# Decode attention with a gated MLP: the MLP's weights loaded first, its gate made ahead of the query projection

## The chip, the cores and the metric

The kernel runs on one core of one Trainium2 chip. The metric is the device time of one execution in microseconds (us), as the median of several runs. A core has engines that run side by side, each with its own instruction stream: TensorE (PE in the profile) for matmuls, VectorE (DVE), ScalarE (ACT), GpSimd (POOL) and SyncE (SP), which here does nothing but issue transfers. Transfers from memory are carried by 16 DMA engines.

## The reference

One step of decoding for 8 sequences, in float32: attention over a cache of 4096 keys and values with 32 query heads on 8 key/value heads, and beside it a small MLP whose output, through a silu, multiplies the attention's output.

```python
xn = _layernorm(x)                                  # x: 8 x 1 x 512
# attention: 32 query heads, 8 key/value heads, 128 wide, 4096 positions
q = (xn @ wq) per head
p = softmax(q @ k_cache^T * 128 ** -0.5)
s = (p @ v_cache) over all heads @ wo               # 8 x 1 x 512
# MLP, F = 1792, Fh = 896
z = _gelu(xn @ w_in)                                # tanh form
z1, z2 = z[..., :Fh], _layernorm(z[..., Fh:])
g = w_sp * z2 + b_sp                                # w_sp, b_sp: one number each
y = (z1 * g) @ w_out
return x + s * _silu(y)
```

The caches are 2 x 134 MB, wq and wo 8.4 MB each, the MLP's weights 5.6 MB. Each byte is used once.

## The kernel before, in words

Three slots of 64 KiB in each of the 128 partitions (`slot_a`, `slot_b`, `slot_c`, 8.39 MB each) take all large transfers. For each of the 8 key/value heads h there are four loads that fill a slot: the keys of sequences 0 to 3 (`kT[h, 0]`, into slot a) and of 4 to 7 (`kT[h, 1]`, slot b), then the values in the same two halves (`v[h, 0]` into a, `v[h, 1]` into b). In this text K0 and K1, V0 and V1 are these four of head 0. Slot c holds wq first, and wo at the end. The MLP's weights share slot b with K1: `w_in`, `w_out` and a last block of 128 columns, `side`, of which only two are used (w_sp and b_sp).

`load` (L130) issues a transfer and makes it count up a semaphore as it lands. All large loads stand on SP's queue, written out in the order in which they are to go: wq, the MLP's weights, K0, K1, V0, V1, the same four of every further head, then wo in six pieces and the residual input. A load into a slot that is still read waits on SP for the last reader, and everything behind it waits too. K1 waits for `gate_made`, the last instruction of the MLP, because slot b holds the MLP's weights till then. V0 waits for the step `k0` (the scores of K0 are made), V1 for `k1`; a later head's first half of the keys for `c0`, its second half for `c3`, the steps after which slots a and b have been read.

Ahead of the loop come, in this order on each engine: the layer norm of x and its transposition into `xnT` (L163 to L172); the query projection (L175 to L195), two rounds of 16 matmuls with wq, each followed by a scaling on VectorE into `q_sb`, four transpositions and a copy into `q_all`, and at the end a copy of head 0's queries into `qz`; and the MLP (L198 to L269): a matmul with w_in, a gelu and a layer norm on VectorE with short steps on ScalarE, GpSimd and TensorE, transpositions, a matmul with w_out, a matmul with `pick` that rearranges the result, and the silu, which ends in `gate`. The MLP's intermediates `z`, `u`, `hT`, `y` and `e` are taken by `scratch` from the front of slot c, over wq, which has been read by then. Both parts use the PSUM tiles `t[0]` and `t[1]`.

Matmuls are in float32, and the trace shows each as two passes. VectorE's, ScalarE's and GpSimd's instructions are all recorded on L48, in the helper `op`; all loads on L133.

The loop over heads on TensorE (L311) makes the scores of a half as it lands (`scores`, L290), waits for the softmax on VectorE and ScalarE, transposes the probabilities (L325), and multiplies them with the values of each half (`values`, L300). After the loop come the output projection with wo (L417, L429, L440), the product with the gate and the sum with x.

Of the kernel before, what the change touches and what calls it, by code (L numbers as in the profile page):

```python
# [5 lines left out]
ALU = mybir.AluOpType  # L6
AX = mybir.AxisListType

P = 128
B, D = 8, 512  # L10
HKV, REP, S, DH = 8, 4, 4096, 128
NK = D // P
G = 4
J = S // (G * P)
R = 32
# [11 lines left out]
WO_PIECES = [(0, 18 * D), (18 * D, 26 * D), (26 * D, 28 * D), (28 * D, 30 * D), (30 * D, LAST), (LAST, NWO * D)]  # L27
FOLDED = NWO - REP
N_IN, N_OUT = NK * 2 * FH, NB * D
N_MLP = N_IN + N_OUT + P  # L30


# [26 lines left out]
def build(nc, x, kT, v, wq, wo, w_mlp, x_res, out):  # L59
    def sb(name, shape, align=32):  # L60
        return nc.alloc_sbuf_tensor(name, shape, F32, align_bytes=align).ap()

    slots = [sb(f"slot{i}", [P, SLOT], 512) for i in range(3)]
    slot_a, slot_b, slot_c = slots
    ident = sb("ident", [P, P])
    x_sb = sb("x_sb", [B, D])
    xn = sb("xn", [B, D])
    xnT = sb("xnT", [P, NK, R])
# [5 lines left out]
    q_sb = sb("q_sb", [P, REP * DH])  # L74
    q_all = sb("q_all", [P, HKV, B, REP])
    qz = sb("qz", [P, B * (R + REP)])
    p = sb("p", [P, J, P])
# [12 lines left out]
    def ps(name, shape):  # L90
        return nc.alloc_psum_tensor(name, shape, F32).ap()
# [4 lines left out]
    t = [ps(f"t{i}", [P, 512]) for i in range(2)]  # L96
# [6 lines left out]
    V = Lane(nc, nc.vector, "v_done")  # L103
# [3 lines left out]
    te = nc.tensor  # L107

    class Marks:
        sem = pe_sem  # L110
        n = 0
    PE = Marks()

    def mark(ins):
        ins.then_inc(pe_sem, 1)
        PE.n += 1
        return PE, PE.n

    def pe_wait(*after):
        for lane, n in after:  # L120
            te.wait_ge(lane.sem, n)
# [5 lines left out]
    def landed(key):  # L127
        return Dma(key), 16

    def load(engine, dst, src, key, *after):  # L130
        for lane, n in after:
            engine.wait_ge(lane.sem, n)
        engine.dma_start(dst, src).then_inc(loaded[key], 16)  # L133


    load(nc.scalar, x_sb, x, "x")
    load(nc.sync, slot_c, wq, "wq")
    load(nc.sync, slot_b[:, :N_MLP], w_mlp, "mlp")
    load(nc.sync, slot_a, kT[0, 0], "a")


# [5 lines left out]
    qz_zero = L.op("memset", qz, 0.0, alone=True)  # L147
# [5 lines left out]
         after=[made])  # L153
# [11 lines left out]
    d = V.op("tensor_scalar", rstd[:, 0:1], mv[:, 1:2], EPS, None, op0=ALU.add)  # L165
    d = L.op("tensor_tensor", rstd[:, 1:2], rstd[:, 0:1], neg_half[:B, 0:1], op=ALU.pow, after=[d])
    d = V.op("tensor_scalar", xn, x_sb, mv[:, 0:1], rstd[:, 1:2], op0=ALU.subtract, op1=ALU.mult, after=[d])
    pe_wait(made, d)
    for k in range(NK):
        i = te.transpose(misc[:, k * B:(k + 1) * B], xn[:, k * P:(k + 1) * P], ident[:B, :B])  # L170
    d = V.op("tensor_copy", xnT[:, :, :B], misc[:, :NK * B].rearrange("p (k b) -> p k b", k=NK),
             after=[mark(i), xnT_zero])  # L172


    wq_v = slot_c.rearrange("p (k n) -> p k n", k=NK)  # L175
    pe_wait(landed("wq"), d)
    for quad in range(2):
        for k in range(NK):
            for g in range(G):
                lo = (quad * G + g) * REP * DH  # L180
                i = te.matmul(t[0][R * g:R * (g + 1), :], xnT[:, k, :], wq_v[:, k, lo:lo + REP * DH],  # L181
                              start=(k == 0), stop=(k == NK - 1))
        d = V.op("tensor_scalar", q_sb, t[0], float(DH) ** -0.5, None, op0=ALU.mult, after=[mark(i)])
        pe_wait(d)
        for r in range(REP):
            i = te.transpose(t[1][:, r * P:(r + 1) * P], q_sb[:, r * DH:(r + 1) * DH], ident)
        tv = t[1].rearrange("p (r g c) -> p g c r", r=REP, g=G)
        V.op("tensor_copy", q_all[:, quad * G:(quad + 1) * G], tv[:, :, :B], after=[mark(i)])
    wq_read = PE, PE.n
    qz_v = qz.rearrange("p (b s) -> p b s", s=R + REP)[:, :, :REP]  # L190

    def next_q(h):
        return V.op("tensor_copy", qz_v, q_all[:, h], after=[qz_zero] if h == 0 else [])

    q_ready = next_q(0)  # L195


    spare = [0]  # L198

    def scratch(n):  # L200
        lo = spare[0]
        spare[0] = lo + n
        return slot_c[:, lo:lo + n]

    w_in = slot_b[:, :N_IN].rearrange("p (k a f) -> p k a f", k=NK, a=2)
    w_out = slot_b[:, N_IN:N_IN + N_OUT].rearrange("p (j d) -> p j d", j=NB)
    side = slot_b[:, N_IN + N_OUT:N_MLP]
    z = scratch(2 * FQ).rearrange("p (a f) -> p a f", a=2)
    u = scratch(2 * FQ).rearrange("p (a f) -> p a f", a=2)
    pz = t[0].rearrange("p (a f) -> p a f", a=2)  # L210
    d = V.op("memset", t[0], 0.0)
    pe_wait(landed("mlp"), d)
    for k in range(NK):
        for g in range(G):
            lo = g * FQ
            n = min(FQ, FH - lo)
            i = te.matmul(pz[R * g:R * (g + 1), :, :n], xnT[:, k, :], w_in[:, k, :, lo:lo + n],
                          start=(k == 0), stop=(k == NK - 1))
# [4 lines left out]
    d = V.op("tensor_mul", uf, uf, zf)  # L223
    d = A.op("activation", uf, uf, AF.Tanh, scale=GELU_C, after=[d])
# [15 lines left out]
    d = V.op("tensor_scalar", one["var"], one["var"], EPS, None, op0=ALU.add)  # L240
    d = L.op("tensor_tensor", one["rs"], one["var"], neg_half, op=ALU.pow, after=[d])
    V.op("tensor_scalar", z2, z2, one["rs"], None, op0=ALU.mult, after=[d])
    V.op("tensor_scalar", z2, z2, side[:, 0:1], side[:, 1:2], op0=ALU.mult, op1=ALU.add, after=[landed("mlp")])
    d = V.op("tensor_mul", u[:, 1, :], z2, z1)
    hT = scratch(2 * P).rearrange("p (a s) -> p a s", a=2)
    pe_wait(d)
    for a in range(2):
        i = te.transpose(t[1][:, a * P:(a + 1) * P], u[:, 1, a * P:(a + 1) * P], ident)
    d = V.op("tensor_copy", hT, t[1][:, :2 * P].rearrange("p (a s) -> p a s", a=2), after=[mark(i)])
    pe_wait(d)  # L250
    for j in range(NB):
        g, a = divmod(j, 2)
        i = te.matmul(t[0][R * g:R * (g + 1), :], hT[:, a, R * g:R * (g + 1)], w_out[:, j, :],
                      start=(a == 0), stop=(a == 1 or j == NB - 1))
    mlp_read = mark(i)
    y = scratch(D)
    d = V.op("tensor_copy", y, t[0], after=[mlp_read])
    pe_wait(d)
    py = misc[:, 128:128 + W]
    for g in range(G):  # L260
        for a in range(2):
            i = te.matmul(py[R * g:R * (g + 1), :], pick[:, a, :],
                          y[:, (2 * g + a) * W:(2 * g + a + 1) * W], start=(a == 0), stop=(a == 1))
    e = scratch(W)
    d = V.op("tensor_scalar", e, py, -1.0, 87.0, op0=ALU.mult, op1=ALU.min, after=[mark(i)])
    d = A.op("activation", e, e, AF.Exp, after=[d])
    V.op("tensor_scalar", e, e, 1.0, None, op0=ALU.add, after=[d])
    V.op("reciprocal", e, e)
    gate_made = V.op("tensor_mul", gate, py, e)  # L269


    STEPS = ["k0", "k1", "a", "mm", "tot", "t0", "t1", "v0", "v1", "c0", "v2", "v3", "c3"]
# [2 lines left out]
    def step(h, name):  # L275
        return PE, base + h * len(STEPS) + STEPS.index(name) + 1
# [34 lines left out]
    with te.Fori(0, HKV):  # L311
# [11 lines left out]
        for c in range(2):  # L323
            for j in range(4):
                i = te.transpose(t[c][:, j * P:(j + 1) * P], p[:, 4 * c + j, :], ident)  # L325
# [21 lines left out]
    def softmax(h):  # L347
        nm, l, w, wl = (one[n] for n in ("nm", "l", "w", "wl"))
        V.op("tensor_reduce", nm, sc, op=ALU.max, axis=AX.XY, negate=True, after=[step(h, "k1")])
        give()  # L350
        A.op("activation", p.rearrange("p j s -> p (j s)"), sc.rearrange("p c s -> p (c s)"), AF.Exp,
             bias=nm, accum_out=l, after=[step(h, "a")])
        V.op("tensor_reduce", nmin, misc[:1, :P].rearrange("b (g r) -> b r g", g=G), op=ALU.min, axis=AX.X,
             after=[step(h, "a")])
        V.op("tensor_copy", row, nmin[:, None, :].to_broadcast([1, G, R]))
        give()
        d = V.op("tensor_sub", w, misc[:, 256:257], nm, after=[step(h, "mm")])
        d = A.op("activation", w, w, AF.Exp, after=[d])
        V.op("tensor_mul", wl, w, l, after=[d])
        give()  # L360
        V.op("reciprocal", wl, misc[:, 320:321], after=[step(h, "tot")])
        V.op("tensor_mul", w, w, wl)
        V.op("tensor_scalar", p, p, w, None, op0=ALU.mult)
        give()
        for c in range(2):
            tv = t[c].rearrange("p (j g i e r) -> p e j i g r", j=4, g=G, i=B // 2, e=2)
            for e in range(2):
                V.op("tensor_copy", pT_v[:, 4 * c:4 * c + 4, :, e, e].rearrange("p j i (g r) -> p j i g r", g=G),
                     tv[:, e], after=[step(h, f"t{c}")] if e == 0 else [], alone=(e == 1))
        if h + 1 < HKV:  # L370
            next_q(h + 1)
        give()
# [7 lines left out]
    for h in range(HKV):  # L380
# [13 lines left out]
        else:  # L394
            for a in range(2):
                o_made = V.op("tensor_copy", oT_last[:, :, a, a * B:(a + 1) * B], po_t,
                              after=[step(h, "c3"), oT_zero] if a == 0 else [], alone=(a == 1))


    for i, (lo, hi) in enumerate(WO_PIECES):  # L400
        load(nc.sync, slot_c[:, lo:hi], wo[:, lo:hi], f"wo{i}", *([gate_made] if i == 0 else []))
    load(nc.sync, x_out, x_res, "res")
    wo_v = slot_c.rearrange("p (m d) -> p m d", d=D)
    part, acc = [sc[:, 0, :D // 2], t[0][:, :D // 2]], sc[:, 1, :W]
# [8 lines left out]
    for m in range(FOLDED):  # L413
        h, r = divmod(m, REP)
        need((m + 1) * D)
        for s in range(2):
            i = te.matmul(part[s][R * r:R * r + B, :], oT[:, h, r, :], wo_v[:, m, s * D // 2:(s + 1) * D // 2],  # L417
                          start=(m < REP), stop=(m >= FOLDED - REP))
# [18 lines left out]
    for g in range(G):  # L437
        for a in range(2):
            c = (2 * g + a) * W
            te.matmul(acc[R * g:R * g + OUT_ROWS, :], pick[:, a, :OUT_ROWS], part_f[:, c:c + W],  # L440
                      start=False, stop=False)
# [8 lines left out]
    d = V.op("tensor_add", gate, gate, x_out, after=[landed("res")])  # L450
# [3 lines left out]
    lo, hi = min(s.num for s in used), max(s.num for s in used)  # L454
# [39 lines left out]
```

## Time and profile before

| | |
|---|---|
| median of 3 runs | 688.91 us (688.72 to 689.17) |
| the profiled execution | 687.01 us, its span from the first to the last instruction 685.7 us |
| moved | 290.97 MB, 424 GB/s on average over the span |
| busy share of the span | TensorE 53%, VectorE 17%, ScalarE 2%, GpSimd 1% |
| mean granted TensorE clock | 0.741 of full speed |

A profile here is one execution recorded by the hardware. Its page gives the busy time of each engine, the span cut into 40 slices (17.14 us each) with the busy share in tenths, what the DMA engines moved in each, the chain of work that ended last, and groups of equal instructions. In rows of instructions the first number is the start in us from the span's start, the second the time to the end of the group, then engine, line, operation, the tiles written and read, the count, and in brackets how long the engine had been idle before it and what ended that. Rows of transfers give the median time from issue to landing.

### The profile page before, as it was taken

How to read it: one execution, taken by the hardware profiler on the slowest of the kernel's cores; microseconds unless marked ns; L12 is line 12 of the kernel's file. 1: busy time of each engine (PE TensorE's matmuls, PEld its weight loads, DVE VectorE, ACT ScalarE, POOL GpSimd, SP SyncE). 2: the span in 40 equal slices, each digit the busy share in tenths (PEclk: the TensorE clock that was granted, in tenths of full speed). 3: DMA queues.
4: the chain of work that ended last, by engine and by line, in shares of the span. 5: the costliest groups of instructions: out<-in, count | busy, mean ns of one | idle time of the engine just before them, and what ended most of it. 6: DMA issues, size and time to landing. Idle time of an engine off the chain costs nothing. (4 is left out here: it accounts for less than half of the span.)

```text
span 685.7 us, 5749 instructions
## 1 busy us (share of the span) xinstructions
PE 361.2 (53%) x2544; PEld 124.2 (18%) x2544; DVE 113.7 (17%) x222; ACT 13.8 (2%) x28; POOL 4.2 (1%) x13
## 2 busy tenths in 40 slices
PE   0637255655644465655645365555644455655637
PEld 0112021211311121211211121211211121211313
DVE  3051022200311022200302022200202022200302
ACT  0000000000000000000000000000000000000000
POOL 2000000000000000000000000000000000000000
PEclk9987666677677667767767767767777676677779
DMA  9996999999999999999999999999999999999997
GB/s 418 398 433 264 460 432 425 428 428 432 428 432 428 428 428 459 443 432 428 432 432 428 432 428 428 451 447 436 428 432 429 428 432 432 428 440 459 436 397 293
DMA packets 6072, 290.97 MB, mean 424 GB/s; under 512 B 936, under 2 KB 1064, under 8 KB 1456
## 3 DMA queue, kind: packets, MB, share of 16 engines
q1 hardware_dynamic: 6048, 290.85, 98.2%
q8 instruction: 5, 0.08, 0.0%
q14 instruction: 3, 0.02, 0.0%
q10 hardware_dynamic: 16, 0.02, 0.0%
HBM read 290.83 MB, written 0.03 MB: 424 GB/s over the span
## 5 line engine op out<-in xcount | busy, mean ns | idle before, releaser
L290 PE MATMUL sc<-slot,qz 128*32 128x512 f32 x1024 | 147.9, 742 | 133.1 <-PEq L282 133.1
L300 PE MATMUL o_ps<-slot,pT 128*32 128x512 f32 x1024 | 151.1, 747 | 98.4 <-PEq L282 98.4
L290 PEld LDWEIGHTS sc<-slot,qz 128*32 128x32 f32 x1024 | 40.5, 133 | 234.0 <-issue 234.0
L300 PEld LDWEIGHTS o_ps<-slot,pT 128*32 128x32 f32 x1024 | 44.3, 130 | 186.5 <-issue 186.4
L48 DVE TENSOR_TENSOR o_all<-o_ps,diag 128x512 f32<-128x512 f32 x32 | 22.1, 692 | 203.9 <-PE o_ps L300 203.9
L48 DVE TENSOR_REDUCE nm<-sc 128x1 f32<-128x1024 f32 x8 | 9.8, 1225 | 278.1 <-PE sc L290 278.1
L48 DVE TENSOR_REDUCE o_sb<-o_all 128x128 f32<-128x512 f32 x32 | 33.6, 1051 | 1.1
L325 PE MATMUL t<-ident,p 128*128 128x128 f32 x64 | 15.5, 424 | 11.7 <-PEq L279 11.7
L48 ACT ACTIVATE p<-sc,nm 128x1024 f32<-128x1024 f32 x8 | 8.9, 1113 | 566.8 <-PE misc L317 566.8
L306 PE MATMUL po<-fold,o_sb 128*128 128x8 f32 x64 | 12.4, 266 | 14.2 <-PEq L279 14.2
L181 PE MATMUL t<-slot,xnT 128*32 128x512 f32 x64 | 10.2, 792 | 14.4 <-DMA slot<-in_wq 14.4
L306 PEld LDWEIGHTS po<-fold,o_sb 128*128 128x128 f32 x64 | 9.7, 190 | 35.8 <-issue 35.8
L325 PEld LDWEIGHTS t<-ident,p 128*128 128x128 f32 x64 | 12.6, 224 | 12.1 <-issue 12.1
L48 DVE COPY pT<-t 128x256 f32<-128x256 f32 x32 | 12.1, 419 | 12.0 <-PE t L325 11.2
L317 PE MATMUL misc<-ident,nm 128*1 128x128 f32 x8 | 2.2, 269 | 12.5 <-PEq L279 12.5
L321 PE MATMUL misc<-wl,same 128*128 128x1 f32 x16 | 3.8, 310 | 8.2 <-PEq L279 8.2
L48 DVE TENSOR_SCALAR p<-p,w 128x1024 f32<-128x1024 f32 x8 | 6.0, 753 | 0.3
L181 PEld LDWEIGHTS t<-slot,xnT 128*32 128x32 f32 x64 | 2.3, 137 | 20.4 <-DMA slot<-in_wq 14.5
L48 DVE TENSOR_SCALAR q_sb<-t 128x512 f32<-128x512 f32 x2 | 1.4, 692 | 24.1 <-PE t L181 24.1
L319 PE MATMUL misc<-ident,row 1*128 1x1 f32 x8 | 1.7, 211 | 6.7 <-PEq L279 6.7
L321 PEld LDWEIGHTS misc<-wl,same 128*128 128x128 f32 x16 | 3.4, 265 | 8.7 <-issue 8.7
L231 PE MATMUL misc<-s,same 128*128 128x1 f32 x4 | 1.2, 362 | 7.0 <-DVE s L48 7.0
(79 smaller groups left out, 71.2 us busy)
## 6 DMA issues: line engine op xcount, KB each, us to landing
slot<-in_w_mlp SPq DMA_DIRECT2D x1, 5440.0 KB, 34.1
slot<-in_wo SPq DMA_DIRECT2D x1, 4608.0 KB, 39.4
slot<-in_wo SPq DMA_DIRECT2D x1, 2048.0 KB, 43.8
slot<-in_wo SPq DMA_DIRECT2D x2, 512.0 KB, 45.0
slot<-in_wo SPq DMA_DIRECT2D x1, 384.0 KB, 45.8
slot<-in_kT SPq DMA_DIRECT2D x16, 27.4
slot<-in_v SPq DMA_DIRECT2D x16, 29.3
slot<-in_wo SPq DMA_DIRECT2D x1, 128.0 KB, 45.7
```

What stands on the lines that cost most here:

```text
L48: ins = getattr(self.engine, name)(*args, **kw)
L181: i = te.matmul(t[0][R * g:R * (g + 1), :], xnT[:, k, :], wq_v[:, k, lo:lo + REP * DH], start=(k == 0), stop=(k == NK - 1))
L231: m = mark(te.matmul(misc[:, col:col + 1], same_all, one[part], start=True, stop=True))
L290: i = te.matmul(sc[R * g:R * (g + 1), c, :], qz[:, b * R:(b + 1) * R], k_v[:, n, c, g, :], start=(b == 0), stop=(b == B - 1))
L300: i = te.matmul(of[R * c:R * (c + 1), :], pT[:, j, 2 * pair + e].rearrange("p e q -> p (e q)"), v_v[:, 2 * (pair % 2) + e, j], start=(j < ...
L306: return te.matmul(po[:, pair * 2 * REP:(pair + 1) * 2 * REP], o_sb[pair % 2], fold.rearrange("p e r -> p (e r)"), start=True, stop=True)
L317: mark(te.transpose(misc[:1, :P], one["nm"], ident))
L319: mark(te.transpose(misc[:, 256:257], row.rearrange("b g r -> b (g r)"), ident[:1, :1]))
L321: mark(te.matmul(misc[:, 320:321], same_all, one["wl"], start=True, stop=True))
L325: i = te.transpose(t[c][:, j * P:(j + 1) * P], p[:, 4 * c + j, :], ident)
```

## The change

Three things are changed.

The MLP's weights are the first load on SP's queue, and wq the second. Of the 10,880 columns of the weights only the `N_USED` = 10,754 that are read are loaded: 126 columns of padding at the end of `side` stay behind.

The code of the query projection stands behind the MLP instead of ahead of it, so that each engine comes to it after its part of the gate.

The MLP's intermediates lie in slot b, behind the place of the weights (from column 10,880 on), since slot c now receives wq while the MLP is computed. wo's first load into slot c waits for the last read of wq (`wq_read`) instead of for the gate.

```diff
+N_USED = N_IN + N_OUT + 2
...
     load(nc.scalar, x_sb, x, "x")
+    load(nc.sync, slot_b[:, :N_USED], w_mlp[:, :N_USED], "mlp")
     load(nc.sync, slot_c, wq, "wq")
-    load(nc.sync, slot_b[:, :N_MLP], w_mlp, "mlp")
     load(nc.sync, slot_a, kT[0, 0], "a")
...
-    wq_v = slot_c.rearrange("p (k n) -> p k n", k=NK)
-    pe_wait(landed("wq"), d)
-    for quad in range(2):
...
-    q_ready = next_q(0)
-
-
-    spare = [0]
+    spare = [N_MLP]
...
-        return slot_c[:, lo:lo + n]
+        return slot_b[:, lo:lo + n]
...
-    d = V.op("memset", t[0], 0.0)
-    pe_wait(landed("mlp"), d)
+    zeroed = V.op("memset", t[0], 0.0)
+    pe_wait(landed("mlp"), zeroed)
...
     gate_made = V.op("tensor_mul", gate, py, e)
...
+    wq_v = slot_c.rearrange("p (k n) -> p k n", k=NK)
+    pe_wait(landed("wq"))
+    for quad in range(2):
...
+    q_ready = next_q(0)
...
-        load(nc.sync, slot_c[:, lo:hi], wo[:, lo:hi], f"wo{i}", *([gate_made] if i == 0 else []))
+        load(nc.sync, slot_c[:, lo:hi], wo[:, lo:hi], f"wo{i}", *([wq_read] if i == 0 else []))
```

On SP, the head of the queue before. Names in brackets are the semaphores an instruction waits for: `v_done` is VectorE's (here the gate), `pe_done` TensorE's.

```order
L133 DMA slot<-in_wq 128x16384 [waits barrier_Pool_Activation_PE_DVE_SP_release]
L133 DMA slot<-in_w_mlp 128x10880
L133 DMA slot<-in_kT 128x16384
L133 DMA slot<-in_kT 128x16384 [waits v_done]
L133 DMA slot<-in_v 128x16384 [waits pe_done] x2
```

And now:

```order
L134 DMA slot<-in_w_mlp 128x10754 [waits barrier_Pool_Activation_PE_DVE_SP_release]
L134 DMA slot<-in_wq 128x16384
L134 DMA slot<-in_kT 128x16384
L134 DMA slot<-in_kT 128x16384 [waits v_done]
L134 DMA slot<-in_v 128x16384 [waits pe_done] x2
```

The first two have changed places, and the weights' rows are shorter; the wait of K1 for the gate stands where it stood.

On TensorE, from the first wait for a large load before (`ld_wq` and `ld_mlp` are the landings):

```order
L181 MATMUL t<-slot,xnT 32x512 [waits v_done,ld_wq]
L181 MATMUL t<-slot,xnT 32x512 x15
L186 MATMUL t<-ident,q_sb 128x128 [waits v_done]
L186 MATMUL t<-ident,q_sb 128x128 x3
L181 MATMUL t<-slot,xnT 32x512 x16
L186 MATMUL t<-ident,q_sb 128x128 [waits v_done]
L186 MATMUL t<-ident,q_sb 128x128 x3
L217 MATMUL t<-slot,xnT 32x512 [waits v_done,ld_mlp]
```

And now, from the end of the MLP on (L231 is the matmul with w_out, L240 that with `pick`, L256 and L261 are the query projection, L291 the first scores):

```order
L231 MATMUL t<-slot 32x512 [waits v_done]
L231 MATMUL t<-slot 32x512 x6
L240 MATMUL misc<-slot,pick 32x64 [waits v_done]
L240 MATMUL misc<-slot,pick 32x64 x7
L256 MATMUL t<-slot,xnT 32x512 [waits ld_wq]
L256 MATMUL t<-slot,xnT 32x512 x15
L261 MATMUL t<-ident,q_sb 128x128 [waits v_done]
L261 MATMUL t<-ident,q_sb 128x128 x3
L256 MATMUL t<-slot,xnT 32x512 x16
L261 MATMUL t<-ident,q_sb 128x128 [waits v_done]
L261 MATMUL t<-ident,q_sb 128x128 x3
L312 UNCONDITIONAL_BRANCH [waits v_done,l_done]
```

The projection stands between the MLP's last matmul and the loop over heads (the branch), where before it stood ahead of the MLP's first matmul.

More of the change, by code (lines that the diff above doesn't have):

```diff
@@ L172, in build @@
              after=[mark(i), xnT_zero])
-    wq_v = slot_c.rearrange("p (k n) -> p k n", k=NK)
-    pe_wait(landed("wq"), d)
-    for quad in range(2):
[L178 to L193, printed above, removed]
-    q_ready = next_q(0)
-    spare = [0]
+    spare = [N_MLP]
     def scratch(n):
@@ L269, in build, with next_q @@
     gate_made = V.op("tensor_mul", gate, py, e)
+    wq_v = slot_c.rearrange("p (k n) -> p k n", k=NK)
+    pe_wait(landed("wq"))
+    for quad in range(2):
+        for k in range(NK):
+            for g in range(G):
+                lo = (quad * G + g) * REP * DH
+                i = te.matmul(t[0][R * g:R * (g + 1), :], xnT[:, k, :], wq_v[:, k, lo:lo + REP * DH],
+                              start=(k == 0), stop=(k == NK - 1))
+        d = V.op("tensor_scalar", q_sb, t[0], float(DH) ** -0.5, None, op0=ALU.mult, after=[mark(i)])
+        pe_wait(d)
+        for r in range(REP):
+            i = te.transpose(t[1][:, r * P:(r + 1) * P], q_sb[:, r * DH:(r + 1) * DH], ident)
+        tv = t[1].rearrange("p (r g c) -> p g c r", r=REP, g=G)
+        V.op("tensor_copy", q_all[:, quad * G:(quad + 1) * G], tv[:, :, :B], after=[mark(i)])
+    wq_read = PE, PE.n
+    qz_v = qz.rearrange("p (b s) -> p b s", s=R + REP)[:, :, :REP]
+    def next_q(h):
+        return V.op("tensor_copy", qz_v, q_all[:, h], after=[qz_zero] if h == 0 else [])
+    q_ready = next_q(0)
     STEPS = ["k0", "k1", "a", "mm", "tot", "t0", "t1", "v0", "v1", "c0", "v2", "v3", "c3"]
```

## The prediction

> **What bounds the kernel now.** I read the page's busy shares and its 40 slices first, to see which resource has no room.
>
> ```profile
> span 685.7 us, 5749 instructions
> PE 361.2 (53%) x2544; PEld 124.2 (18%) x2544; DVE 113.7 (17%) x222; ACT 13.8 (2%) x28; POOL 4.2 (1%) x13
> DMA  9996999999999999999999999999999999999997
> GB/s 418 398 433 264 460 432 425 428 428 432 428 432 428 428 428 459 443 432 428 432 432 428 432 428 428 451 447 436 428 432 429 428 432 432 428 440 459 436 397 293
> q1 hardware_dynamic: 6048, 290.85, 98.2%
> ```
>
> TensorE is busy half of the time, the other engines less. The transfers fill nine tenths or more of every slice but two: the last, and the fourth, which spans 51.4 to 68.6 us. So the kernel is one long stream of loads on SP's queue (q1) with one hole in it. Against the 430 GB/s around it, the fourth slice lost (430 - 264) x 17.14 us = 2.8 MB, or 6.6 us.
>
> I then asked what SP, which issues the loads, waited for, and when it issued the first ones.
>
> ```profile
> SPq L133 <- DVE gate L48: 57.4, 1, 57.4
> 0.74 0.38 SPq L133 DMA_DIRECT2D slot<-in_wq  x1
> 1.17 0.43 SPq L133 DMA_DIRECT2D slot<-in_w_mlp  x1
> 59.49 0.33 SPq L133 DMA_DIRECT2D slot<-in_kT  x1
> ```
>
> The second half of head 0's keys ("K1"; K0 is the first, V0 and V1 the values) goes into slot b, where the MLP's weights lie until the gate is made. SP stands at that wait from about 2 us to 59.49.
>
> The stretches around the hole show its ends (the last two columns are DMA share and GB/s; a packet counts where it starts, hence shares over 1).
>
> ```profile
> 48.00:52.00 4.00, 0.98 (x4) 0.79 (x4) 1.88 (x6) 0.00 (x0) 0.56 (x1) 0.50 1.21 524
> 52.00:53.00 1.00, 0.41 (x6) 0.12 (x8) 0.42 (x1) 0.00 (x0) 0.00 (x0) 0.50 0.00 0
> 53.00:54.00 1.00, 1.00 (x8) 0.31 (x11) 0.00 (x0) 0.00 (x0) 0.00 (x0) 0.50 0.18 66
> 54.00:60.00 6.00, 2.84 (x30) 0.73 (x27) 1.89 (x5) 0.26 (x1) 0.00 (x0) 0.78 0.01 1
> 60.00:61.00 1.00, 1.00 (x8) 0.23 (x5) 0.00 (x0) 0.00 (x0) 0.00 (x0) 0.50 3.16 1049
> ```
>
> 1049 GB/s over 1 us is 16 packets of 64 KiB, one per DMA engine: K1 begins in 60 to 61. Before it only one packet (66 GB/s for 1 us) starts after 52. That one packet matters below: one engine of the 16 ends K0 late.
>
> **The price of the hole.** The queue's landings (us from issue; the first three transfers, then K1) and the starts of TensorE's groups that wait for a load:
>
> ```profile
> slot<-in_wq SPq DMA_DIRECT2D x1, 21.8
> slot<-in_w_mlp SPq DMA_DIRECT2D x1, 5440.0 KB, 34.1
> slot<-in_kT SPq DMA_DIRECT2D x1, 54.6
> slot<-in_kT SPq DMA_DIRECT2D x1, 21.8
> 81.38 9.56 PE L290 MATMUL sc<-slot,qz 128*32 128x512 f32 x64 [13.16 <-PEq L282]
> 101.77 9.67 PE L300 MATMUL o_ps<-slot,pT 128*32 128x512 f32 x64 [2.93 <-PEq L282]
> 121.58 6.52 PE L300 MATMUL o_ps<-slot,pT 128*32 128x512 f32 x32 [9.83 <-PEq L282]
> 160.23 9.39 PE L290 MATMUL sc<-slot,qz 128*32 128x512 f32 x64 [10.50 <-PEq L282]
> 624.24 9.49 PE L290 MATMUL sc<-slot,qz 128*32 128x512 f32 x64 [10.40 <-PEq L282]
> 662.84 5.55 PE L300 MATMUL o_ps<-slot,pT 128*32 128x512 f32 x32 [10.53 <-PEq L282]
> ```
>
> wq lands at 0.74 + 21.8 = 22.5, the MLP's weights at 1.17 + 34.1 = 35.3, K0 at 1.6 + 54.6 = 56.2, K1 at 59.5 + 21.8 = 81.3. From head 1 to head 7 the same wait ends at 160.23 and 624.24: 24 loads in 464.0 us, 19.33 us each (8.39 MB, 434 GB/s). In an unbroken stream K0 would have landed at 35.3 + 19.3 = 54.6 on all engines but the late one, and K1 at 74.0. It came at 81.3 or 81.4: the hole costs 7.4 us. (The slices gave 6.6; they don't see that the first packets after the hole take 3.16 us, by the share of 3.16 for 16 packets, where the stretch 48 to 52 has 2.42: 1.21 x 4 us x 16 engines over 32 packets.)
>
> **The change, part by part.**
> *Order of the loads.* The same three transfers go out back to back on SP, in another order, and nothing else on SP is passed. The MLP's weights take 35.3 - 22.5 = 12.8 us beside wq's 19.33, so the first load carries 22.5 - 19.3 = 3.2 us of start, and the weights land at 3.2 + 12.7 = 15.9. wq lands at 35.2, K0's bulk at 54.5. Until there it is worth 0.
> *Shorter rows.* 126 of 10,880 columns stay behind: 126 x 4 x 128 = 64,512 B, at 434 GB/s 0.15 us, a gain. Rows of 43,016 B out of a pitch of 43,520 have no equal in this trace. The nearest is wo's first piece, rows of 36,864 B from a pitch of 65,536:
>
> ```profile
> 634.17 2.80 SPq L133 DMA_DIRECT2D slot<-in_wo  x6
> slot<-in_wo SPq DMA_DIRECT2D x1, 4608.0 KB, 39.4
> ```
>
> It lands at 634.2 + 39.4 = 673.6, 10.8 us after V1 of head 7 (662.8), 437 GB/s: the pitch costs nothing, and I take -0.15. What it lacks is the odd length (8 bytes over a multiple of 512), a rival below. The Trainium skill ("DMA: Bandwidth & Descriptors", How a descriptor splits into AXI transactions) says that a 256-byte-aligned descriptor goes as pieces of 256 B and a leftover piece; by that the row falls from 170 pieces to 169, and the gain would be nearer 0.08 than 0.15 us. No row here shows a leftover.
> *The gate ahead of the query projection.* The chain from which I take the times:
>
> ```profile
> 22.55 6.53 PE L181 MATMUL t<-slot,xnT 128*32 128x512 f32 x32 [14.41 <-DMA slot<-in_wq]
> 30.56 3.64 PE L181 MATMUL t<-slot,xnT 128*32 128x512 f32 x32
> 36.18 0.18 DVE L48 COPY qz<-q_all 128x32 f32<-128x32 f32 x1
> 37.17 3.63 PE L217 MATMUL t<-slot,xnT 128*32 128x512 f32 x32 [1.42 <-DVE t L48]
> 57.11 0.46 PE L262 MATMUL misc<-slot,pick 128*32 128x64 f32 x16 [0.92 <-DVE slot L48]
> 59.23 0.23 DVE L48 TENSOR_TENSOR gate<-misc,slot 128x64 f32<-128x64 f32 x1
> 59.81 8.41 PE L290 MATMUL sc<-slot,qz 128*32 128x512 f32 x64 [2.24 <-PEq L282]
> ```
>
> The same 32 passes take 6.53 us after a long idle time and 3.64 right behind it. Now the MLP's come first, so I give them 6.53 for 3.63 (with 3.63 the gate is 2.9 us sooner; nothing hangs on it). From their end (40.8) to the end of the gate (59.46) were 18.7 us. The gate is made at 15.9 + 6.5 + 18.7 = 41.1, and K1 can be issued there, 13 us before K0's stream ends at 54.5. The hole is closed; its 7.4 us are the gain.
> *The query projection behind it.* TensorE is through with the gate at 41.1 - 1.9 = 39.2 (59.46 - 57.57 = 1.9) and wq is there since 35.2. From its first pass to qz it took 22.55 to 36.36, 13.8 us; so qz is ready at 53.0. K0's last engine lands at about 56, so this lies beside the load and costs 0. Queued behind it on TensorE are the scores of K0, and on SP, V0's load, which waits until they have been read from slot a. They take 8.4 to 9.6 us: 56 + 9.6 = 65.6, and V0's packets are needed when K1's stream ends at 73.8. Cover 8 us.
> *The scratch in slot b, wo's wait.* Same shapes in the same memory, no transfer; K1 waits for the gate already. wo's first piece waits on the last read of wq instead of the gate; SP comes to it at 634 us, past both. Each 0.
>
> **What the hole hid.** With it gone, what is late next? K0's late engine. In 42 to 43 and 112 to 113 us instruction blocks (q8) pass through the DMA engines:
>
> ```profile
> q8 instruction: 1, 0.02, 5.9%
> q8 instruction: 1, 0.02, 5.5%
> ```
>
> K0's landing is 56.2 - 54.6 = 1.6 us late, K0 being in flight at 42; I read it as the engine that carried the block. At the hole all engines start anew, so that lateness is forgiven. Two later blocks show what stays: V0 comes 101.77 - (81.38 + 19.33) = 1.06 late, V1 121.58 - (81.38 + 38.66) = 1.54 late, and this is never made up (19.33 per load from there on). Two delays of 1.06 and 1.54, not 1.06 + 1.06, speak for different engines each time. In the new kernel the 1.6 of K0's engine stays too; if it is a third engine the end waits for the largest, 1.6 against 1.54, a loss of 0.1. If it is one of the two, for their sum, a loss of up to 1.6. I take 0.1.
>
> **Sum.** -7.4 - 0.15 + 0.1 = -7.45, rounded to -7.4 us. Head 7 and the tail hang on the stream (V1 at 662.84, then wo's pieces), so all of it reaches the end. The profiled execution took 687.01 us (span 685.7 and 1.3 around it) and should take 679.6. The median of the runs, 688.91, lies 1.9 above it; minus 7.4 it gives 681.5. A change within 0.2% (1.4 us) can't be told from none.
>
> **Rivals.**
> 1. *The late engines add up.* The block of K0 meets an engine that a later block meets too: gain 5.8 to 6.0, time 683.0. For it: nothing forgives any more. Against it: the two later blocks met different engines. The Trainium skill ("DMA: Bandwidth & Descriptors", Queues, rings and completion order) says each DMA engine takes turns between its queues packet by packet, so a block delays its one engine's loads; the late landing of K0 agrees. "Runtime: NRT & Kernel Launch" (Instruction fetch mechanics) calls the fetch hidden; by that the loss is 0, and K0's late landing speaks against it. 10 in 100.
> 2. *The hole moves behind K1.* If qz came late, V0 would be issued late. Decides from 73.8 - 1 (issue to first packet, 59.49 to 60 or 61) - 9.6 = 63.2 for qz; I have 53.0. With every TensorE pass of the projection at the slow rate (3.64 becoming 6.53) it is 55.9. A chain 5 us longer yet than that would cost nothing; one of 15 us more (68) costs 5, time 686. 4 in 100.
> 3. *Slower: the odd rows.* Were the first load slow because its rows are no multiple of 512 B, all behind it would shift. It decides where the load takes 12.7 + 7.4 = 20.1 us instead of 12.7 (274 GB/s), and 21.5 for slower by 0.2%. At half its rate (25.4) the time is 688.9 - 7.4 + 12.7 = 694.2. Against it: wo's cut rows at 437 GB/s. 3 in 100.
> 4. *It doesn't do what it says:* the gate still comes after K0, because its chain is longer when it starts early. It would need 27 us from weights to gate to become 39. 688.9; 2 in 100.
>
> **How the numbers follow.** My forecast has 81 in 100. Its own range is 680.4 to 682.4: upward 0.8 if the hole is worth the slices' 6.6 and not 7.4; downward 0.1 if K0's late engine costs nothing, some 0.45 as the runs spread (688.72 to 689.17), and 0.5 because the runs' offset from a profile (1.9) need not stay. The high end of the whole range, 683.8, takes in rival 1 (683.0) with the same 0.8. Together that is 91 in 100, less for what I have not thought of. Faster by over 0.2%: forecast, rival 1 and most of rival 2, 0.95. Same: rival 4, 0.02. Slower: rival 3, 0.03.
>
> **What would show it.** The new trace should have no slice under 9 tenths but the last; K1's issue near 41 (right if before 53); K1's landing at 74 to 76 and V1's of head 0 near 114; the MLP's 32 passes from 15.9 at about 6.5 us; K0's scores starting at the landing of K0 and not later; head 7's last wait at 655.4 for 662.84. Wrong it is if the loads of a head no longer come every 19.33 us, if DMA is idle between K1 and V0, if the first load takes much over 13 us after its start, or if head 7's landing is more than 2 us behind the bulk.

## The result, and the profile after

| | before | changed |
|---|---|---|
| median of 4 runs each, same chip | 688.82 us (688.35 to 689.17) | 680.61 us (680.25 to 682.64) |
| the profiled execution | 687.01 us, span 685.7 | 680.59 us, span 679.1 |

The ratio is 0.9892, 95% interval 0.9874 to 0.991. Forecast were 681.5 us, and -7.4 us; measured were -8.2 between the medians and -6.4 between the two profiled executions. Why these two differ by more than the forecast missed is the second half of what follows.

The page of the changed kernel: the same rows as shown of before.

```profile
span 679.1 us, 5748 instructions
DMA  9999999999999999999999999999999999999996
GB/s 387 432 433 433 433 432 432 433 432 432 436 448 432 444 440 432 441 432 432 432 432 432 432 432 432 432 432 432 432 444 433 432 432 432 432 432 432 432 421 268
q1 hardware_dynamic: 6048, 290.79, 99.0%
```

The hole in the fourth slice (264 GB/s) is gone: 433 there now, and no slice but the last is under nine tenths.

SP's first issues, its wait for the gate, and the landings of the first four transfers:

```profile
0.74 0.38 SPq L134 DMA_DIRECT2D slot<-in_w_mlp  x1
1.17 0.42 SPq L134 DMA_DIRECT2D slot<-in_wq  x1
39.73 0.33 SPq L134 DMA_DIRECT2D slot<-in_kT  x1
SPq L134 <- DVE gate L49: 37.3, 1, 37.3
slot<-in_w_mlp SPq DMA_DIRECT2D x1, 5377.0 KB, 15.3
slot<-in_wq SPq DMA_DIRECT2D x1, 34.2
slot<-in_kT SPq DMA_DIRECT2D x1, 54.1
slot<-in_kT SPq DMA_DIRECT2D x1, 35.4
```

The weights land at 0.74 + 15.3 = 16.0, wq at 35.4, K0 at 1.64 + 54.1 = 55.8. K1 goes out at 39.73, 16 us before K0 has landed, and lands at 39.7 + 35.4 = 75.1, where it came at 81.3 before.

TensorE's groups from the first weights to head 0's values, and at head 7:

```profile
16.07 5.00 PE L195 MATMUL t<-slot,xnT 128*32 128x512 f32 x32 [7.93 <-DMA slot<-in_w_mlp]
37.36 0.46 PE L240 MATMUL misc<-slot,pick 128*32 128x64 f32 x16 [0.92 <-DVE slot L49]
37.60 3.64 PE L256 MATMUL t<-slot,xnT 128*32 128x512 f32 x32
47.22 0.66 PE L261 MATMUL t<-ident,q_sb 128*128 128x128 f32 x4 [0.89 <-DVE q_sb L49]
55.90 8.99 PE L291 MATMUL sc<-slot,qz 128*32 128x512 f32 x64 [8.03 <-PEq L283]
75.22 9.57 PE L291 MATMUL sc<-slot,qz 128*32 128x512 f32 x64 [10.32 <-PEq L283]
113.90 5.59 PE L301 MATMUL o_ps<-slot,pT 128*32 128x512 f32 x32 [10.50 <-PEq L283]
655.95 5.92 PE L301 MATMUL o_ps<-slot,pT 128*32 128x512 f32 x32 [10.17 <-PEq L283]
```

The gate is ready before K0 has landed, the query projection runs right behind it, and K0's scores begin at 55.90, when K0 has landed and not later. V1 of head 0 starts 7.68 us sooner than before (121.58), V1 of head 7 only 6.89 us sooner (662.84). So 0.8 us of the gain are given back between these two.

### The profile page after: what moved, and what is told of

The parts are those of the page before. It is cut to its first block, busy times and chain, and to the rows that moved or that the text cites. A ratio compares the mean times of both kernels' runs of the same rounds, so it can differ in the third digit from the quotient of the medians.

```text
span 679.1 us, 5748 instructions
## 1 busy us (share of the span) xinstructions
PE 352.8 (52%) x2544; PEld 122.3 (18%) x2544; DVE 113.7 (17%) x222; ACT 13.8 (2%) x28; POOL 4.2 (1%) x13
## 5 line engine op out<-in xcount | busy, mean ns | idle before, releaser
L291 PE MATMUL sc<-slot,qz 128*32 128x512 f32 x1024 | 145.2, 730 | 143.3 <-PEq L283 143.3
L301 PE MATMUL o_ps<-slot,pT 128*32 128x512 f32 x1024 | 147.8, 732 | 98.0 <-PEq L283 98.0
L291 PEld LDWEIGHTS sc<-slot,qz 128*32 128x32 f32 x1024 | 40.0, 131 | 242.2 <-issue 242.2
L195 PE MATMUL t<-slot,xnT 128*32 128x512 f32 (+1 forms) x32 | 5.0, 729 | 7.9 <-DMA slot<-in_w_mlp 7.9
L256 PE MATMUL t<-slot,xnT 128*32 128x512 f32 x64 | 7.3, 594 | 0.0
L418 PE MATMUL sc<-slot,oT 128*8 128x256 f32 x56 | 4.5, 379 | 0.4 <-DVE oT_last L49 0.4
L49 DVE COPY slot<-t 128x512 f32<-128x512 f32 (+1 forms) x3 | 1.8, 603 | 16.5 <-PE t L195 12.1
## 6 DMA issues: line engine op xcount, KB each, us to landing
slot<-in_w_mlp SPq DMA_DIRECT2D x1, 5377.0 KB, 15.3
```

What stands on the lines that cost most here:

```text
L49: ins = getattr(self.engine, name)(*args, **kw)
L291: i = te.matmul(sc[R * g:R * (g + 1), c, :], qz[:, b * R:(b + 1) * R], k_v[:, n, c, g, :], start=(b == 0), stop=(b == B - 1))
L301: i = te.matmul(of[R * c:R * (c + 1), :], pT[:, j, 2 * pair + e].rearrange("p e q -> p (e q)"), v_v[:, 2 * (pair % 2) + e, j], start=(j < ...
```

## The experiments

Two questions: is the hole all there is, and does each half of the change close it alone? And what makes the gain at head 7, the gain of the profile and the gain of the medians differ? Each kernel was timed beside the kernel before on the same chip.

**Loads only, code only, and K1 held back.** Four kernels, timed in one sitting; the kernel before was at 688.41 us there.

*e1:* the kernel before with the two first loads exchanged.

```diff
-    load(nc.sync, slot_c, wq, "wq")
     load(nc.sync, slot_b[:, :N_MLP], w_mlp, "mlp")
+    load(nc.sync, slot_c, wq, "wq")
```

> The kernel before with one edit: the MLP's weights are loaded ahead of wq; code order, row length and scratch as before. Theory A (the gain is the hole in the stream, and only the gate's time sets it): wq lands at 35.3, the query projection takes 13.8 to 49.1, the MLP 23 more, so K1 goes out near 72.3 and lands near 94 instead of 81.3: slower than before by about 12.8 us, near 701.6. Theory B (the order of the loads is itself worth something, the stream runs better when the small load comes first): between 681 and 689.

Measured: 701.32 us, ratio 1.0197 (1.018 to 1.0214). SP's queue and the page's GB/s:

```profile
SPq L133 <- DVE gate L48: 70.1, 1, 70.1
GB/s 380 454 446 1 361 421 420 451 443 420 428 443 450 420 428 428 461 421 431 420 458 431 431 420 446 443 424 428 439 450 421 428 424 465 424 428 424 458 405 283
```

The gate comes behind a projection that now waits for the second load; the hole fills a whole slice (1 GB/s) and part of the next. The order of the loads by itself costs 12.9 us, as theory A said to 0.3 us.

*e2:* the changed kernel with wq loaded first again.

```diff
-    load(nc.sync, slot_b[:, :N_USED], w_mlp[:, :N_USED], "mlp")
     load(nc.sync, slot_c, wq, "wq")
+    load(nc.sync, slot_b[:, :N_USED], w_mlp[:, :N_USED], "mlp")
```

> The changed kernel with one edit: wq is loaded first again, the MLP's weights second (short rows, scratch in slot b and the new code order stay). Theory A: the weights land at 35.2, 5.0 us of passes and 18.7 us of chain follow, the gate is made near 59.0, K1 goes out 0.5 us earlier than before, qz is ready near 68 and V0 goes out near 77, before K1's stream ends at 80: time 688.3, within 0.8 us of before. Theory B (making the gate ahead of the projection is worth something without the loads): 681 to 685.

Measured: 688.92 us, ratio 1.001 (0.9999 to 1.0021), so within 0.8 us of before: without the loads' order no gain can be seen. K1 went out at about 59.4, as before. Only both halves together bring the gate ahead of K0's end.

*e3 and e4:* the changed kernel, with K1 held back by one more wait.

```diff
-            load(nc.sync, slot_b, kT[h, 1], "b", gate_made)
+            load(nc.sync, slot_b, kT[h, 1], "b", gate_made, q_ready)          # e3
+            load(nc.sync, slot_b, kT[h, 1], "b", gate_made, step(h, "k0"))    # e4
```

> The changed kernel with one edit: K1's load waits for head 0's queries (near 48.7 us) as well as for the gate (39.7). Theory A: it still goes out before K0's stream ends near 54.3, so the time is that of the changed kernel, 680.6, within 0.5. Theory B (an earlier issue of K1 as such is worth something, the DMA queues run better when filled long ahead): later by up to 9 us, 681.5 to 689.

> The changed kernel with one edit: K1's load waits for the scores of K0 (near 65.0 us). Theory A: a hole from 54.3 to 66; K1 lands at 65.0 + 21.8 = 86.8 where its bulk landed at 73.7 and its last engine at 75.1, so 11.7 to 13.1 us over the changed kernel: 692.3 to 693.7; from the kernel before, whose K1 went out 5.5 us sooner, 694.2. Theory B (part of the 8.2 us comes from the shorter rows or the new order and not from the hole): below 692, by as much as that part is.

Measured: e3 680.92 us, as the changed kernel; e4 693.04 us, inside theory A's 692.3 to 693.7. An issue of K1 10 us later (49.8) is free while K0 is still in flight, and costs its full length once it is not. Holding K1 back gives away all of the gain and more, though the loads' order, the short rows and the scratch are the changed kernel's. So theory A holds, and the gain is the hole.

**The late engines.** Of each load the 16 DMA engines report their landings one by one. The distance of each from the first, in us, for V1 of head 7, as the traces of the profiled executions have it:

| kernel | first lands at | 16 engines, us behind the first |
|---|---|---|
| before | 660.87 | 13 within 0.35; 1.21, 1.65, 1.84 |
| changed | 653.14 | 12 within 0.43; 1.37, 1.43, 1.44, 2.68 |
| changed, second profile | 653.21 | 12 within 0.63; 1.47, 1.49, 1.51, 2.56 |
| e5, loop written out | 653.11 | 7 within 0.40; 7 at 2.68 to 3.16; 4.42, 4.62 |

Counted by the first engine the change brings 7.73 us at head 7, counted by the last 6.89. To see whether the instruction blocks make the late ones, *e5* writes TensorE's loop out, so that it fetches more of them.

```diff
-    with te.Fori(0, HKV):
+    for _ in range(HKV):
         take_load("a")
...
-    assert PE.n == base + len(STEPS)
-    PE.n = base + HKV * len(STEPS)
+    assert PE.n == base + HKV * len(STEPS)
```

> The changed kernel with TensorE's loop over heads written out, so that it fetches its program in some 16 more blocks of 16 KiB during the stream. Theory A (each block makes the DMA engine that carries it 1.0 to 1.6 us late, and that is never made up): more and more engines are late from head to head; if the blocks spread evenly the whole stream ends about 1 us later, 681.5; where they meet the same engine twice or three times the last landing is 3 to 5 us behind the bulk, 682 to 685. Theory B (the late engines have another cause): landings as in the changed kernel, 680.6, within 0.5.

The blocks between 100 and 660 us, in the changed kernel and then in e5:

```profile
q8 instruction: 1, 0.02, 0.0%
q8 instruction: 16, 0.26, 0.2%
```

Measured: 682.08 us, against 680.61 and 680.39 for the changed kernel: some 1.5 us more. The intervals of the ratios to the kernel before overlap (0.9896 to 0.9932 here, 0.9874 to 0.991 and 0.9882 to 0.9913 there), so it is the landings that decide: seven engines are not touched, seven are about 3.0 us late and two 4.5. These are two and three times 1.5, so a block makes the engine that carries it about 1.2 to 1.6 us late, hardly any of that is made up, and the blocks come back to the same engines rather than going evenly over all 16. Theory A holds; its even spread does not.

*e6*, a single run of the changed kernel with all 10,880 columns loaded:

```diff
-    load(nc.sync, slot_b[:, :N_USED], w_mlp[:, :N_USED], "mlp")
+    load(nc.sync, slot_b[:, :N_MLP], w_mlp, "mlp")
```

> The changed kernel with all 10,880 columns of the MLP's weights loaded. Theory A: the weights land 0.15 us later than in the changed kernel (its bulk at 15.7, its last engine at 16.0), the time 0.1 to 0.2 more, which one look can't tell. Theory B (a row that is no multiple of 512 bytes costs something): the weights land earlier although they are more.

The first wait for the weights ended at 16.19, beside 16.07 in the changed kernel and 16.40 in its second profile: the odd rows cost nothing that can be seen, and the shorter ones gain nothing that can be told from the start's spread. The time was 684.0 us, 3 us more than rows could explain. The rows of its tail, V1 of head 7 and the first group of the output projection, show what did. In the row of a stretch of time the third figure from the end is the granted clock:

```profile
656.12 6.47 PE L301 MATMUL o_ps<-slot,pT 128*32 128x512 f32 x32 [9.62 <-PEq L283]
668.62 0.51 PE L307 MATMUL po<-fold,o_sb 128*128 128x8 f32 x2 [1.78 <-PEq L280]
669.57 1.06 PE L418 MATMUL sc<-slot,oT 128*8 128x256 f32 x8 [0.44 <-DVE oT_last L49]
670.38 1.10 PE L418 MATMUL t<-slot,oT 128*8 128x256 f32 x8
668.00:676.00 8.00, 6.94 (x70) 3.04 (x74) 0.71 (x3) 0.00 (x0) 0.00 (x0) 0.57 0.64 256
```

and the same place in the changed kernel's profile:

```profile
668.69 0.64 PE L418 MATMUL sc<-slot,oT 128*8 128x256 f32 x8 [0.43 <-DVE oT_last L49]
669.12 0.64 PE L418 MATMUL t<-slot,oT 128*8 128x256 f32 x8
668.00:676.00 8.00, 7.35 (x173) 4.52 (x177) 0.71 (x3) 0.38 (x1) 0.00 (x0) 1.00 0.63 252
```

V1 landed at the same time in both (656.1 and 655.9). From 668 to 676 the granted clock was 0.57 in the one and 1.00 in the other, and groups of the output projection took 1.06 to 1.10 us instead of 0.64. The two executions differ by TensorE's clock in the tail, after the last V1. The other profiles fit: that of e3 (682.59 us) has three slow groups of the output projection at this place, those of the changed kernel (680.59 and 680.58 us) none.

**TensorE kept busy.** If that is what sets runs apart, work in TensorE's idle time should bring them together. The first try had too much of it.

```diff
         mark(combine(0))
+        for _ in range(28):
+            te.matmul(po[:, 256:], ident, pT_w, start=True, stop=True)
         take_load("b")
```

> The changed kernel with work added: in each head 28 matmuls on constants into unused columns of po, about 8 us, while TensorE waits for V1, so that it is not idle when V1 lands. Theory C (the tail after the last V1 is TensorE's chain, slowed by its clock after 10 us of idling, and this phase makes the runs differ): the first pair's values take 3.7 us instead of 5.9, and the end moves until wo's last piece (landing at 675.4 of a span of 679.1) binds: 0.6 us less in an execution like the profiled one, up to 2.6 less in one like that of e3 (6.5 us and three slow groups of the output projection); median 678.9 to 680.2, runs closer together. Theory D (the late landings alone set the end, and differ between runs): 680.6, within 0.5.

> The kernel before with the same 28 matmuls per head. Theory C: the first pair's values of head 7 take 3.7 us instead of 5.6, 0.4 us less in an execution like the profiled one (687.0) and more in slower ones: median 686.5 to 687.8, and the distance to the changed kernel with the same addition is the stream's alone, 7.4 plus or minus 0.5. Theory D: 688.4, within 0.5, and the distance stays 8.2.

Measured: 681.78 and 688.55 us, neither better, and the runs no closer (679.55 to 682.95; 685.37 to 690.91). Two rows of w_after, at head 7, tell why:

```profile
646.21 12.33 PE L335 MATMUL po<-pT,ident 128*128 128x256 f32 x56
658.47 3.68 PE L301 MATMUL o_ps<-slot,pT 128*32 128x512 f32 x32
```

The 28 matmuls took 12.3 us, not 8, and the idle time is 10: the values began 2.6 us after V1 had landed (655.84). They did run at full speed (3.68), but the output projection, behind TensorE's next wait of 1.78 us, began with slow groups of 1.06 to 1.10 us again. My size was wrong, and the time says nothing for or against theory C. The second try has 20 of them, and 3 more ahead of the last combine, where TensorE waits 1.8 us.

> The changed kernel with 20 matmuls on constants per head while TensorE waits for V1 (8.8 us of its 9.6 to 10 us of idle time; the 28 of w_after took 12.3 and made it late) and 3 more in its wait of 1.8 us ahead of the last combine. Theory C (the tail is TensorE's chain, slowed by its clock): values of the first pair in 3.7 us, no slow group in the output projection, the end within 1 us of wo's last landing: median 679.0 to 680.2, no run above 681. Theory D (landings alone): 680.6 to 680.9, and runs of 682 stay.

> The kernel before with the same additions. Theory C: 686.3 to 687.5, runs close together, and the distance to v2_after is the stream's alone: the hole (7.4), the rows (0.15), less 0.1 to 1 for late engines that are no longer made up: 6.5 to 7.5. Theory D: 688.0 to 688.6, and a distance of 8.2.

> The changed kernel once more, for its spread and a second look at the late engines. Theory A: K0's late engine stays late to the end, so four engines are late at the last V1 where the kernel before has three. Theory C: runs between 680.2 and 684, the median 680.6 to 681.2; the slower of two profiles is the one whose clock was at half in more of the tail.

| | median | runs | ratio to the kernel before |
|---|---|---|---|
| kernel before, this sitting | 687.42 | 17, 686.42 to 688.66 | |
| v2_before | 686.91 | 12, 685.87 to 688.34 | 0.9996 (0.9986 to 1.0006) |
| changed kernel again | 680.39 | 5, 679.83 to 681.25 | 0.9897 (0.9882 to 0.9913) |
| v2_after | 679.66 | 4, 679.47 to 679.83 | 0.9887 (0.987 to 0.9905) |

The tail of v2_after, its clock from 656 to 676, and the output projection:

```profile
655.96 3.68 PE L301 MATMUL o_ps<-slot,pT 128*32 128x512 f32 x32 [1.35 <-PEq L283]
656.00:662.00 6.00, 6.00 (x54) 2.24 (x58) 1.79 (x2) 0.00 (x0) 0.00 (x0) 1.00 0.92 399
662.00:676.00 14.00, 12.24 (x218) 6.93 (x210) 2.44 (x5) 0.39 (x1) 0.00 (x0) 1.00 0.78 322
666.85 0.64 PE L423 MATMUL sc<-slot,oT 128*8 128x256 f32 x8 [0.81 <-DMA slot<-in_wo]
```

V1 landed where it did in the changed kernel (655.95), but the first pair's values take 3.68 us for 5.92, the clock is 1.00 throughout, and the output projection now waits for wo: the tail is bound by the transfers again. The changed kernel's runs spread over 1.4 us here and 2.4 in the first sitting, v2_after's over 0.36. So for the changed kernel theory C holds, with the reserve that 4 and 5 runs are few. For the kernel before it is not borne out: v2_before is within its interval of no change, and its 12 runs still spread over 2.5 us. Part of the spread of the kernel before lies outside the span: in 3 of its 17 runs the time is 2.0 to 2.8 us above the span, where 1.3 to 1.6 is usual, and in none of v2_before's. The spans of the two still spread over 2.2 and 2.4 us; what varies there stays open. The distance between the two is 7.25 us, inside the 6.5 to 7.5 expected of the stream alone. v2_after is faster than the kernel before by 7.8 us and than the changed kernel by 0.7 by the medians; none of its runs is slower than the fastest of the changed kernel, though the two intervals overlap.

## Why the prediction was right, point by point

*The bound and the hole.* Right. Its price of 7.4 us, from one load each 19.33 us and K1's landing, is borne out by the first engine's landings, which come 7.17 us sooner at K1 and 7.73 at head 7 (with the rows' 0.15 in it), and by V1 of head 0 (7.68, where the kernel before had its own late engines). The slices' 6.6 was too low, as the text said.

*The gate's chain.* Right in kind, 1.4 us too late: K1 went out at 39.73, not 41.1. The MLP's 32 passes took 5.00 us; I had taken the 6.53 of the projection's first round, and e1 shows 6.51 for that round after 27 us of idle time. From the weights' landing to the gate it was 23.7 us, where the sum has 25.2 and rival 4 speaks of 27. The cover was 13 us, so nothing hung on it.

*The query projection behind it.* Right, and too dear: 37.60 to about 48.7 is 11.1 us, not 13.8, since TensorE came to it with its clock up (both rounds 3.64). K0's scores began when K0 landed.

*Shorter rows.* -0.15 us was in the sum and can't be seen; nor can a cost. The estimate of 0.08, worked out from the Trainium skill ("DMA: Bandwidth & Descriptors", How a descriptor splits into AXI transactions), stays undecided: starts at 16.07, 16.40 and, with full rows, 16.19 spread more than that. It also counts the leftover piece of 8 B as a whole one, which the section doesn't say.

*The late engines.* This is the term that was mis-sized: +0.1 forecast, +0.8 measured at head 7. That an engine made late stays late was right. What the prediction overlooked is a second kind of block. Besides the block of 16 KiB of queue q8 near 42 us, one of 8 KiB of another instruction queue, q14, passes three times in each profile. In the kernel before, the first of these came at 59.6 us, in the hole. The row of that queue for 59 to 60 us:

```profile
q14 instruction: 1, 0.01, 3.1%
```

All of K1's landings then lay within 0.54 us. In the changed kernel it came at 51.7, with K0 in flight, and K0 landed with two late engines, 1.61 and 1.24 us behind the first. e2 bears this out: there q8's block came at 58.2, in the hole, and q14's at 73.3, and K0's landings lay within 0.61 us, while K1 had one late engine (1.13). So the changed kernel has four late engines where the one before has three.

From head 1 to head 5 this cost about what was forecast: at the landings of K1 and V1 the last engine was 1.4 to 2.0 us behind the first, where before it was 1.6 to 1.7. But the later blocks of q14 met an engine that was late already. At 514 to 515 us the changed kernel's profile has the third:

```profile
q14 instruction: 1, 0.01, 1.9%
520.85 8.63 PE L291 MATMUL sc<-slot,qz 128*32 128x512 f32 x64 [8.76 <-PEq L283]
```

The last engine went from 1.85 to 2.79 us behind, and the load that TensorE waited for at 520.85 came 20.28 us after the one ahead of it instead of 19.3. The trace does not number the engines, but the distances tell which one it was: the 1.24 of K0 had come down to 1.02 by the end of head 2, became 1.95 at head 3, with the second block (284 us), and was the 1.85 that became 2.79, while the three others stayed at about 1.4. In the kernel before, only two such blocks counted. The last one there took an engine from 0.99 to 1.95 us, too, but another had been at 1.64, and so it cost the load 0.3 us. Rival 1 thus came true by half its size, and through a block that the hole had hidden. Over all profiles the difference is less sharp: at the last V1 the last engine is 2.24 to 2.77 us behind the first in the seven without written-out loop in which all three blocks count, and 1.68 to 2.26 in the five in which a hole makes up for the first.

"Runtime: NRT & Kernel Launch" (Instruction fetch mechanics) in the Trainium skill calls the fetch mostly hidden. Whether an engine waits for its own instructions no run here measures; but in a kernel bound by its loads the DMA engine that carries a block pays, as e5 shows (the last engine 4.62 us behind the first, for 2.68).

*What stood behind the runs.* The text took the offset of 1.9 us between a profile and the median as a constant. It is none: the changed kernel's profile lay on its median (680.59 and 680.61). So it is in part luck that the median came within 0.9 us of the forecast. The profiled execution was 1.0 us slower than forecast (680.59 for 679.6), mostly by the late engines, and the missing offset of 1.9 went the other way. From the wait for the last V1 to the end of the span were 22.9 us before and 23.2 after, and e6 shows that the clock in this stretch can move it by 3 us. The distance of the medians was 8.2, 7.5 and 7.0 us in three sittings (688.82 - 680.61; 688.41 - 680.92 of e3, which is as good as the changed kernel; 687.42 - 680.39). The spans differ less: by 6.6 between the two profiles, and by 7.05 and 6.8 between the medians of the second and third sitting (686.4 and 679.35, 685.9 and 679.1). The rest is time outside the span, which in 6 of the 30 runs of the kernel before there (and in one of e3's four) was 2.0 to 2.8 us, for 1.3 to 1.6 in the others. With the late engines at their measured size the sum is -7.4 - 0.15 + 0.8 = -6.75. So about 7 us is a fair value of the change, and 8.2 is at the high end.

*The rivals that end elsewhere.* The hole behind K1 did not come (qz at 48.7 for a limit of 63.2), nor slow rows. e2 shows what rival 4 would have looked like.

*The signs.* K1's issue and landing (39.73 and 75.1), V1 of head 0 (113.90), the slices and the start of K0's scores came as set down. Head 7's last wait ended at 655.95 for 655.4. One of the signs of being wrong did come: at head 7 the last engine landed 2.68 us behind the first and over 2 behind the bulk, which lay within 0.43. It belongs to the late engines, and not to the hole.

## What to carry to other kernels

In a kernel that is one stream of loads, find the one wait in which the stream's issuer stands, and reorder what stands ahead of it: the work that frees a buffer goes first, both in the loads and in the code. Here either half alone was worth nothing or cost 12.9 us, so try them together. Once the stream has no hole, small things decide the rest: single DMA engines that an instruction block made late, which a hole had forgiven, and the clock of TensorE in the tail after the last load.

## What the runs showed of the hardware that was not expected

A late DMA engine stays late: in a queue that never runs empty, a block of 16 KiB on one engine makes that engine's landings 1.2 to 1.6 us late, a block of 8 KiB 0.9 to 1.0. Hardly any of it is made up (the 1.61 us of K0 in the changed kernel were still about 1.4 at the last V1), and the load counts as landed with its last engine. A hole makes it up at once: in the kernel before K0's last engine was 2.1 us behind the first, and K1's 0.54. In e5, 18 blocks of 16 KiB and 3 of 8 KiB met 9 engines and left 7 alone.

TensorE's granted clock fell to half in the tail of e6 at 668.7 us, right behind a wait of only 1.78 us that followed some 4 us of work at full clock, and stayed there for 6.8 us, in which seven groups ran slowly. In the changed kernel's profile the same wait left it at 1.00.
